# A gated mix of a convolution and a feed-forward net: first products over 512 tokens, another order of loads and of the merged work

## The chip, the core and the metric

The kernel runs on one core of a Trainium2 chip. The core has five engines that run side by side, each through its own list of instructions: TensorE (PE, matrix products, with weight loads shown apart as PEld), VectorE (DVE), ScalarE (ACT), GpSimd (POOL) and SyncE (SP, which here issues most DMAs). The metric is the device time of one execution in microseconds. Times of the kernel before are the median of 3 runs.

## What is computed

```python
x = A_u                                              # 1 x 2048 x 640
g = sigmoid((x * gate_w).sum(-1, keepdims=True))
a = A_ref(x, ...)     # S4D: a kernel K of 2048 taps for each of 640 channels,
                      # convolved with x by Fourier transforms, plus x * D_skip
b = relu(x @ w1) @ w2 # w1 640 x 1728, w2 1728 x 640
return g * a + (1 - g) * b
```

Three kinds of work follow from this: the generation of the taps K (exponentials and sines of 640 x 128 parameters), the convolution, and the feed-forward net `b`. Products are taken in three terms, with each operand split into a rounded part (`h`) and the rest (`l`): high x high, high x low, low x high.

## The kernel before

**Tiles and sweeps.** The hidden dimension of 1728 is cut into 13 tiles of 128 and one of 64. `PARTS = (5, 5, 4)` makes three sweeps `p` of 5, 5 and 4 tiles over all tokens; partial sums go to DRAM between sweeps. Tokens come in eight groups `g` of 256. For a group, first products (`hidden` or `wide`) give the hidden tiles, which ACT (`high`: relu, rounded) and DVE (`low`: the rest) evict from PSUM; second products (`sums`, four blocks j of 320 columns by 128 tokens) give the output.

**First sweep.** `hidden` (line 390) takes one group of 256 tokens and up to two tiles at a time; the hidden tiles are `h0`, `h2`, `h4`. The 64-wide tile (tile 13) is tile 0 of this sweep (line 248): its weights carry high and low side by side, so it needs two products in place of three, and a chain `fold`, `total`, `half_high`, `half_low` over ACT and DVE adds them. **Second and third sweep:** `wide` (line 453) takes 512 tokens, a pair of groups, one tile at a time. Rings in `ring(...)` count the buffers; `Token`s take and release them.

**x and the weights.** `load_x` (line 313) brings a group from DRAM, `trans` (line 335) transposes it on PE in three thirds of the model dimension, and ACT and DVE split it into `xx`. In the first sweep the transposes of group g+1 stand between the products of group g. `weights` (line 257) loads and splits w1 and w2; in the first sweep w1 comes as one load of 64 columns and two of 256. All of these loads are issued by SP.

**The parameters** (`params`, line 719) take 75 DVE steps, some ACT casts, stores to DRAM and loads of rows (`load_rows`), before the first block of the generation (`products`, line 910: PE on `tg,PS`) can start. Later come `factors` and `taps` (generation) and the stages of the convolution (`stage1`, `stage2`, `inv2`, `inv1`).

**The order** is written out by hand: every task is put in a queue such as `PE.ff` or `DVE.prma`, and the string `ORDER` (line 47) says from which queue the next task is taken, one letter a task (a digit repeats it). Each engine runs its tasks in that order. `Plan.run` (line 161) follows it, so nearly every instruction of the profile has line 185.

Of the kernel before, what the change touches and what calls it, by code (L numbers as in the profile page):

```python
# [11 lines left out]
F32 = mybir.dt.float32  # L12
# [16 lines left out]
HB = 1  # L29
# [17 lines left out]
ORDER = (  # L47
    '!PD;T4;mD;Da;Fan;Dn;aBmnmDBDcDBDmDmBD2a2naDnDBaDmDBmDnDBm2DBaDanDmnDBmW2DaBDanDnC2DaCDC!DCDa?2D?DaufuDS2uD2u'
    'DvaDv2Du!vDuDuvDaDa2uD2uDuDu2nDv2aDnDanDanDn3D2anDnv2DuDvaD2uDvDuveDCfDCDuD!DuWD2auDZaDvDuZD?uDvDaDa2nDu2aDn'
    'DnDvDuDavDanDu2DnD2avDnDnDw?DawDuDvDavDwDCgDCDu!DwD:DugD;Du;Du;DaWuD2aDauvDw2DuwuD2nDwauDwauDnanaDnDn2DawenD'  # L50
    'vaDv2DavDuDvWDawWngDvDwDvWDWvDf2Dava2DlWDW2DaDanlnDYDaYDanZnDZP2DaDanDnDEanDCbDCDbD!aDEnaoDbCDCbDo!bDtDt?DE?'
    'bpDpbpDbDpDbDpDaDpabp3DpDaoE2anGnbYbDqbt2DtDaDanDanDaoDbn2DnDabnDpEbpDpb2DpbDpDpDpaE2apDbDobGobn2tEqDbrpUDpb'
    'DpaDbDpDUDbpDbp2Dp2DpaE2aCGbroUbotDbD2nZDqZt2DU?aDananDYanDEnabnDpDbpDpDb2DpbDpbDpDp2DapaE2arDobCDbCDCbGont?'
    'EbtDpbDp2DpbDbp2DmspDbq2D2pDaDaEpamDb2nDsaoaDoGbtanbnEtDnBDbp;DBb2Dr;pbD,pDUbDpaDabpDpDUZpUDaDpmDmBEmoaG;b2B'
    'b;DUobqDqDtDbtDpDbpErbpUDbp2DbpDUZp;DpDmpD2aDnEaBmG;bBo;bDoYbtYDnXDnQDqbDpDrmtDmpDmBDaBDBDa!nDbnEXbspDQbDpDU'
    'bDpD2pDUDrpUEDobDbo!D2sbnDnUnG2tbnEpbDpbp2Dbq2DpbDoDpDpEpDbpDbnDnbDnoG2tbEqbDpb2rDU2pDbDbpDYDpZDpDpEpDboDboG'
    'nbtZtE;q2UDb2pDbpDbDspDbDpbDpDpDpD2aDnaEanGobYnXbnXDqbtDtDoDbpDpbE!pDabUDnDspb2DbpDpDpDpEDobnDnbGnb2tEoDbprp'
    'DUbpDbDpDb!DpbDpDp2DnqEZpDUb2rDUoboDbtGt2U2nEbpDpbpUDbDpbDpDbpDp2DqEnpDbnDboGZobYtXEqDrb2stDbpDpXbDpDbDpbDpD'
    'pDpD2aEpaDbYnUDobDnbDoGtUntbEpbD2pb2DpaDnDaDbnDpbDpDp2DpEnGnbrtUboDobqDtU!DEbp!DrpbUpDbDnbDnDpUb2DpDpDpDpEDn'
    'bnoDboDbDnqDrDtUbGt2bEUZpDpbnDpbDZp;D;DpDpEpDbpDbDoaDobG2tqEbnqDbpDpbDpDmpDmDmpDbBDapDarpU2DapDbDsn;DsnXDsnD'  # L60
    'aDnEtGrboBb;DbtUXDoUDqDrbpDpDb2UpDbDpmDUpDnD2nDnDpZDp2DpDBDB;Gn;nXDqDrsU2DnDUP2KQDQDnmDPmBZDmz;DzKzKQzDQz2Dz'
    'RDmzDaz2DaD2KzQDzQDBD.BDa.zD.DzXDsBDnDanL2nLAKAKADz2DzDzLALADRD2sAD!DADAD!DszDdDdnDndH2ndnH2hyHhyhDhyNhyDNDN'
    'yDNyHNHN2hyHhyhDhyNhyDNDnNnDyNDyHnNHhNhyIhyhyLNyNIA2NLA3iAIiA2LAIRADA2iZDAiZDiZDxZx2DaDnD2xHxH2hyHhyhHhyNhDy'
    'N2hDNyXDNyaDyNDyN-DxNxDNQxHanQHn2hyHhyhHhyNhJyh2NyNyJjyjOIhNyI+NKiN+iNizQKdzDiQdDzDXz2DKa!jnKz!LzdVLzdDA2DAD'
    'ADADL2nLAZDADA2DADMnDInIZQD2iDQiDiDVxD-xDRxDxDxDzDODM2n+DnHnx+Hh-hyHhyhZHhyNhyHN2hZNDy2hNyDxNDxNDyDyHyaNjyNH'
    'nhNHhy+hNhJyX2hyXNyNJjNyNyjINOI-K2iDizQiDzdKdONLzQzK+AD+A2Dz-KjzQLzjL+zdQLAdDRaADADVDAVDAIAIHiD2hyiDyiDinNDa'
    'xDMxHMxa!xNHhn+hHn!2hxDhyhDyDyNDxNDyDxDNxDNnDnHnyZHhyhHyN2hyJN2hNyNyHN2yJNhjyjOIhyI-Ki+2izKQizDOQzDjNDz+LNnN'
    'L+ANZLALAjDVADVAD-DAXDAMDKAMKzD2nDzDI2zInH2iH2hyHiyhiHyN2hHyN2hxDhOhyhNDy+NDxDNx+DNyZDyHyNyHNhnhNHy2hZNxDhyh'
    'DyN-DyaNDxNDyNDxyIxNIxNnJ3iIjIiOjJi-2iDXi+xDaxDdOxDdxDx-DxDx+DxjDn-DOD-Jj+2anJ+n-Dj2DOjVDVDO+3D+M2DVMDnVnj2D'
    'njDOnDdDMdM+DMk2DkZMnZDnDMDnMDk2ZDnkZ')  # L70
# [135 lines left out]
class Kernel:  # L206
# [29 lines left out]
    def feed_forward(self):  # L236
# [6 lines left out]
        for f in range(2, 5):  # L243
            ring(f"hw{f}", 1)
        for f in range(5):
# [11 lines left out]
        def weights(p, f, two, after=()):  # L257
# [7 lines left out]
            def load():  # L265
                if first:
                    n = 256 if f else fn
                    t = st['ws', key] = self.prm.tile([128, NT, n], F32, name=f"wq{f}")
                    D_.dma_start(t, io['B_w1'][:, f0:f0 + n].rearrange("(k p) f -> p k f", p=128))
                    if f:  # L270
                        st['ws', key], st['ws', (key[0], p, f + 1)] = t[:, :, :128], t[:, :, 128:]
# [1076 lines left out]
```

## Time and profile before

| | us |
|---|---|
| median of 3 runs | 611.13 (610.20 to 612.08) |
| the profiled execution | 611.85 |
| its span, first to last instruction | 610.1 |

```profile
PE 598.8 (98%) x8676; PEld 496.4 (81%) x8676; DVE 504.8 (83%) x841; ACT 379.7 (62%) x599; POOL 83.9 (14%) x114
...
PE   6999999999999999999999999999999999999996
PEld 6999998999998998898898896686757846757676
DVE  3788967899999999999998995898878867978542
ACT  4434458999999898899988852133352354343552
POOL 0000000000000000000000000016340360544525
PEclk9899999999999999999999999999999999999999
```

The first line is the busy time of each engine, its share of the span and its instructions. The rows below cut the span into 40 equal slices; a digit is the busy share in tenths, and `PEclk` the clock that TensorE was granted. PE is busy from the first slices to the last. The generation lies between about 94 and 368 us, where ACT and DVE are near full too; the convolution follows.

### The profile page before, as it was taken

How to read it: one execution, taken by the hardware profiler on the slowest of the kernel's cores; microseconds unless marked ns; L12 is line 12 of the kernel's file. 1: busy time of each engine (PE TensorE's matmuls, PEld its weight loads, DVE VectorE, ACT ScalarE, POOL GpSimd, SP SyncE). 2: the span in 40 equal slices, each digit the busy share in tenths (PEclk: the TensorE clock that was granted, in tenths of full speed). 3: DMA queues.
4: the chain of work that ended last, by engine and by line, in shares of the span. 5: the costliest groups of instructions: out<-in, count | busy, mean ns of one | idle time of the engine just before them, and what ended most of it. 6: DMA issues, size and time to landing. Idle time of an engine off the chain costs nothing.

```text
span 610.1 us, 20050 instructions
## 1 busy us (share of the span) xinstructions
PE 598.8 (98%) x8676; PEld 496.4 (81%) x8676; DVE 504.8 (83%) x841; ACT 379.7 (62%) x599; POOL 83.9 (14%) x114
## 2 busy tenths in 40 slices
PE   6999999999999999999999999999999999999996
PEld 6999998999998998898898896686757846757676
DVE  3788967899999999999998995898878867978542
ACT  4434458999999898899988852133352354343552
POOL 0000000000000000000000000016340360544525
PEclk9899999999999999999999999999999999999999
DMA  9767746406154824554155257982946969642376
GB/s 225 198 214 257 201 155 216 159 20 230 67 164 157 255 93 156 192 168 136 66 202 154 59 169 227 259 182 103 211 105 251 186 188 185 217 124 87 84 211 188
DMA packets 85697, 102.56 MB, mean 168 GB/s; under 512 B 28009, under 2 KB 68841, under 8 KB 85354
## 3 DMA queue, kind: packets, MB, share of 16 engines
q1 hardware_dynamic: 85210, 100.39, 55.9%
q8 instruction: 68, 1.11, 0.8%
q10 hardware_dynamic: 400, 0.90, 0.5%
q14 instruction: 19, 0.16, 0.1%
HBM read 62.21 MB, written 39.06 MB: 166 GB/s over the span
## 4 chain that ended last, share of the span: by engine, by line
PE 91%; DMA 3%; SPq 2%; POOL 1%; ACT 1%; issue 1%; DVE 0%; POOLq 0%; ACTq 0%
PE ps L185 91%; SPq L185 2%; DMA xu<-in_A_u_dram 1%; DMA out_dram<-yo 1%; POOL yo L185 1%; POOL q L185 1%; DMA xu<-part 1%; ACT yo L185 0%; ACT L185 0%; ACT mg L185 0%; ACT ku L185 0%; ACT q L185 0%; DVE q L185 0%; POOLq L1344 0%; ACTq L185 0%
## 5 line engine op out<-in xcount | busy, mean ns | idle before, releaser
L185 PE MATMUL ps<-xx,w1h 128*128 128x256 f32 (+1 forms) x760 | 185.3, 341 | 0.5 <-ACT xx L185 0.5
L185 PEld LDWEIGHTS ps<-xx,w1h 128*128 128x128 f32 x760 | 125.9, 191 | 22.5 <-issue 4.2
L185 POOL TENSOR_TENSOR ku<-kx 128x256 f32<-128x256 f32 x80 | 56.7, 738 | 462.5 <-DMA xu<-in_A_u_dram 408.4
L185 PE MATMUL ps<-xx,w1l 128*128 128x512 f32 (+1 forms) x340 | 116.2, 342 | 0.0
L185 ACT COPY ku<-ps 128x256 f32<-128x256 f32 (+1 forms) x120 | 47.9, 472 | 73.0 <-PE ps L185 72.6
L185 PE MATMUL ps<-w2h,hh 128*128 128x320 f32 x288 | 91.2, 320 | 0.0
L185 PE MATMUL ps<-w2l,hh 128*128 128x320 f32 x288 | 87.7, 308 | 0.4 <-issue 0.4
L185 DVE STREAM_TRANSPOSE ku<-ps 128x512 f32<-128x512 f32 x80 | 75.7, 1057 | 11.5 <-PE ps L185 11.4
L185 PE MATMUL ps<-w2h,hl 128*128 128x320 f32 x256 | 73.1, 311 | 0.0
L185 PEld LDWEIGHTS ps<-xx,w1l 128*128 128x128 f32 x340 | 65.0, 191 | 7.4
L185 DVE TENSOR_TENSOR kx<-ps,ku 128x512 f32<-128x512 f32 x80 | 50.6, 681 | 14.0 <-ACT ku L185 8.3
L185 PEld LDWEIGHTS ps<-w2h,hh 128*128 128x128 f32 x288 | 54.1, 188 | 8.4 <-DVE ku L185 2.8
L185 ACT ACT_TABLE_LOAD x42 | 53.9, 1283 | 0.7
L185 PEld LDWEIGHTS ps<-w2l,hh 128*128 128x128 f32 x288 | 54.1, 188 | 0.2
L185 DVE TENSOR_TENSOR mg<-mg,sc 128x1024 f32<-128x1024 f32 x40 | 49.0, 1225 | 3.6
L185 ACT COPY sc<-ps 128x1024 f32<-128x1024 f32 x40 | 40.3, 1008 | 16.7 <-PE ps L185 16.7
L185 DVE TENSOR_TENSOR sc<-sc,mg 128x1024 f32<-128x1024 f32 x40 | 48.6, 1216 | 0.0
L185 PEld LDWEIGHTS ps<-w2h,hl 128*128 128x128 f32 x256 | 46.5, 188 | 1.4 <-issue 0.9
L185 ACT ACTIVATE sc<-sc,half_pi 128x1024 f32<-128x1024 f32 x40 | 45.5, 1138 | 0.0
L185 ACT ACTIVATE sc<-sc 128x1024 f32<-128x1024 f32 x40 | 42.1, 1052 | 0.2
L185 ACT ACTIVATE mg<-ps 128x1024 f32<-128x1024 f32 x40 | 41.7, 1041 | 0.2
L185 PE MATMUL ps<-w2h,xu 128*128 128x320 f32 x160 | 39.7, 310 | 0.0
(161 smaller groups left out, 1090.0 us busy)
## 6 DMA issues: line engine op xcount, KB each, us to landing
xx<-xt SPq DMA_DIRECT2D x24, 640.0 KB, 8.2
xt<-xx SPq DMA_DIRECT2D x16, 640.0 KB, 6.6
part<-q SPq DMA_DIRECT2D x16, 640.0 KB, 4.3
q<-part SPq DMA_DIRECT2D x16, 640.0 KB, 5.5
ws<-in_B_w_dram SPq DMA_DIRECT2D x20, 320.0 KB, 4.1
kd<-kt SPq DMA_DIRECT2D x80, 64.0 KB, 2.8
ck<-kd SPq DMA_DIRECT2D x40, 128.0 KB, 3.4
xu<-in_A_u_dram SPq DMA_DIRECT2D x10, 512.0 KB, 8.2
```

The source lines that it names most:

```text
L185: return lambda *a, **k: self._tc.keep_in_program_order(f(*a, **k))
```

## The change

The diff does four things.

- **512 tokens from the third group on.** In the first sweep groups 0 and 1 keep `hidden`; groups 2 to 7 go through `wide` in pairs, in the order of tiles 4, 0, 1, 2, 3. `wide` learns the 64-wide tile (two products, then the fold chain for each half of the 512 tokens) and gets buffers in the first sweep: `h0` and `h2` as before, a new tile `h5`, two tiles of the convolution's `ck`, and `h4`. The transposes of a pair stand behind the pair before; they have queues of their own (`PE.tr`, `ACT.tr`, `DVE.tr`).
- **The half tile of w1 last.** The first sweep's tiles are now 0, 1, 2, 3, 13; w1 comes as loads of 128, 256, 128 and 64 columns.
- **The first x in three parts.** `load_first` issues each third as two DMAs, one on SP and one on ACT, with the first load of w1 between the second and the last third. In the first group the products of tiles 0 and 1 are split by term, so that the high x high term needs only the high parts.
- **A new merge order.** The whole string `ORDER` is replaced. It begins, in words: first two thirds of x, w1, last third, gate vector, the other w1 loads, second x, w2; on PE the transposes of x, all products of the first group, the transposes of the second group, its sums. The first block of the generation now stands in the products of groups 4 and 5, behind the first of the second tile's five steps; before, it stood behind all products of group 4.

```diff
-        nf = [(i * 128, min(128, DFF - i * 128)) for i in (13, *range(13))]
+        nf = [(i * 128, min(128, DFF - i * 128)) for i in (0, 1, 2, 3, 13, *range(4, 13))]
...
-                    n = 256 if f else fn
+                    n = 256 if f == 1 else fn
...
+        def load_first():
+            s_, ls = tok('xs'), []
+            for third in range(3):
+                def load(third=third):
+                    st['xs', 0], d = self.xu[:, 0], slice(256 * third, min(256 * third + 256, D))
+                    for h in range(2):
+                        (S if h else D_).dma_start(st['xs', 0][64 * h:64 * h + 64, :, d], xd[h, :, :2, d])
+                ls.append(A('SP', 'x0', load, take=() if third else [s_], use=[s_] if third else ()))
+            return s_, ls
...
+                if g == p == i == 0:
+                    nm = 2 if halves(p, f) else 3
+                    for m in range(nm):
+                        for third in range(3):
+                            new = r == third == m == 0
+                            x = X[0, 0][2 * third + (m == 1)]
+                            ts.append(A('PE', 'ff', early(r, f, third, m), [*(wt if nm == 2 else [wt[m == 2]]), x], take=[b_] if new else (),
+                                        use=[w_, xtok[0, 0]] + ([] if new else [b_])))
+                    continue
...
+                if p == 0 and f == 2:
+                    return [self.zp.tile([128, 512], F32R, name=f"h{x}5") for x in 'hl']
+                if p == 0 and f == 3:
+                    return [self.early.tile([128, 16, 32], F32R, name="ck", bufs=2).rearrange("p a b -> p (a b)") for _ in range(2)]
+                if p == 0:
+                    return [pa.tile([128, 2, 256], F32R, name="h4", bufs=1).rearrange("p a b -> p (a b)")]
...
-                    for m, (a, b) in enumerate(((wh, xh), (wh, xl), (wl, xh))):
-                        self.E.matmul(st['hb', 'w'], a[:, k], b, start=k == m == 0, stop=k == NT - 1 and m == 2)
+                    for m, (a, b) in enumerate(((wh, xh), (wh, xl), (wl, xh))[:nm]):
+                        self.E.matmul(st['hb', 'w'], a[:, k], b, start=k == m == 0, stop=k == NT - 1 and m == nm - 1)
...
+            if nm == 2:
+                x = ()
+                for t in range(2):
+                    z_ = tok('z')
+                    x = A('ACT', 'ff', lambda t=t: fold(t), [*ts, *x], take=[z_], use=[b_])
+                    x = A('DVE', 'ff', lambda t=t: total(t), [x], use=[b_, z_])
+                    x = A('ACT', 'ff', lambda t=t: half_high(t), [x], take=() if t else hs, use=[z_, *hs] if t else [z_])
+                    x = A('DVE', 'ff', lambda t=t: half_low(t), [x], use=[z_, *hs]),
...
-                q_ = tok('q')
+                q_, pair = tok('q'), p or g > 1
...
-                for k_, i in enumerate(range(0, 0 if p else n, 2)):
+                for i in () if pair else (4, 0, 2) if g else (0, 2, 4):
                     hidden(p, g, i, range(i, min(i + 2, n)))
...
+                if p == 0:
+                    for i in (1,) if g == 0 else (2, 3) if g == 1 else (g + 2, g + 3) if g % 2 == 0 and g < 6 else ():
+                        for third in range(3):
+                            trans(i, third, xs[i])
+                        if i < 7:
+                            xs[i + 1] = load_x(i + 1, [wload[0, PARTS[0] - 1, 1]])
```

More of the change, by code (lines that the diff above doesn't have):

```diff
@@ L297, in low @@
                 V.tensor_sub(l, t, w.bitcast(F32))
-            if first and f and f % 2 == 0:
+            if first and f == 2:
                 a, s_ = wload[p, f - 1, two], wq[f - 1]
@@ L423, in total, with room @@
                 V.tensor_add(st['z'], st['hb', i][:64, 0], st['z'])
+            def room():
+                if i < 4:
+                    st['h', i] = [pa.tile([128, 2, 256], F32R, name=f"h{x}{i}", bufs=1) for x in 'hl']
+                else:
+                    t = pa.tile([128, 2, 256], F32R, name="h4", bufs=1)
+                    st['h', i] = [t[:, x:x + 1] for x in range(2)]
             def high():
-                st['h', i] = [pa.tile([128, len(fs), 256], F32R, name=f"h{x}{i}", bufs=1 if i else HB) for x in 'hl']
+                room()
                 S.activation(st['h', i][0][:, lo:], st['hb', i][:, lo:len(fs)], AF.Relu)
@@ L433, in half_high @@
             def half_high():
+                room()
                 S.activation(st['h', i][0][:64, 0], st['z'], AF.Relu)
@@ L497, in sums @@
             ts_, ns = slice(t * 128, t * 128 + 128), slice(nh * 320, nh * 320 + 320)
-            if p:
-                hd, ht = zip(*HW[p, g // 2])
+            pair = p or g > 1
+            if pair:
+                hd, ht = zip(*(HW[p, g // 2][f] for f in range(n)))
+                ht = [x for y in ht for x in y]
             else:
```

124 lines of the change are left out of this document (72 added, 52 removed), and 17 rows, old and new, of the table QUEUES.

## The prediction

> **What bounds the kernel now.** I read the chain that ended last first, because it says which engine sets the time in each stage. Its pieces are start, length and what ran.
>
> ```profile
> span 610.1 us, 20050 instructions
> ...
> 14.91 79.74 PE ps L185 x609
> ...
> 98.13 269.87 PE ps L185 x4309
> ...
> 368.36 187.29 PE ps L185 x2859
> ```
>
> From 14.91 us to 555.65 us the chain is matmuls with almost nothing between them. The time is therefore the sum of what TensorE (PE) executes, plus the start and the few waits. A change counts by how much PE time it removes and by the waits it makes. Next I asked how close the other engines are, stage by stage. The columns after the span of each stretch are its length and the busy time of PE, weight loads, VectorE (DVE), ScalarE (ACT) and GpSimd, then clock and DMA.
>
> ```profile
> 5.13:8.55 3.42, 2.61 (x16) 1.79 (x16) 0.65 (x2) 1.43 (x3) 0.00 (x0) 1.00 1.10 287
> 8.55:11.96 3.41, 2.91 (x23) 2.58 (x22) 3.02 (x6) 2.22 (x4) 0.00 (x0) 1.00 1.12 297
> 11.96:15.37 3.41, 1.49 (x14) 1.32 (x12) 1.59 (x4) 2.42 (x5) 0.00 (x0) 1.00 0.99 236
> 15.37:18.79 3.42, 3.42 (x18) 3.42 (x17) 3.16 (x5) 2.56 (x4) 0.00 (x0) 0.50 1.10 342
> ...
> 27.60:85.65 58.05, 58.05 (x445) 57.81 (x444) 49.56 (x109) 25.34 (x53) 0.00 (x0) 1.00 0.65 211
> 93.77:156.14 62.37, 61.28 (x1003) 57.42 (x1002) 56.06 (x100) 59.85 (x76) 0.00 (x0) 1.00 0.42 143
> 156.14:226.05 69.91, 69.91 (x1123) 62.65 (x1117) 68.03 (x114) 65.61 (x77) 0.00 (x0) 1.00 0.50 155
> ```
>
> The first generation stage (93.77 to 156.14) has ACT busy for 59.85 of 62.37 us, the second DVE for 68.03 of 69.91. PE is the bound there by only 2 us. In the start the DMA engines are full until 12 us, PE was idle for over half of 11.96:15.37, and the next stretch ran at clock 0.50.
>
> **The change part by part.** All sums go against the profiled execution, 611.85 us (span 610.1 and 1.75 around it); the median of the runs is 611.13, 0.72 lower, and the forecast is put there.
>
> *First: 512 tokens at once.* Six of the eight groups of the first sweep are affected. Each had 4x15 + 10 = 70 matmuls of 256 columns (the half tile has two products), so 420 become 210 of 512 columns. What one of each costs is the distance of starts:
>
> ```profile
> 31.13 1.60 PE L185 MATMUL ps<-xx,w1h 128*128 128x256 f32 x12
> 32.57 0.28 PE L185 MATMUL ps<-xx,w1l 128*128 128x256 f32 x1
> ...
> 181.76 0.63 PE L185 MATMUL ps<-xx,w1h 128*128 128x512 f32 x2
> ...
> 182.45 0.63 PE L185 MATMUL ps<-xx,w1h 128*128 128x512 f32 x2
> ...
> 229.73 0.62 PE L185 MATMUL ps<-xx,w1h 128*128 128x512 f32 x2
> 230.19 0.39 PE L185 MATMUL ps<-xx,w1l 128*128 128x512 f32 x1
> 230.41 0.62 PE L185 MATMUL ps<-xx,w1h 128*128 128x512 f32 x2
> ...
> 232.23 0.39 PE L185 MATMUL ps<-xx,w1l 128*128 128x512 f32 x1
> 232.54 0.50 PE L185 MATMUL ps<-tg,PS 32*128 32x512 f32 x4
> ...
> 233.32 0.73 PE L185 MATMUL ps<-xx,w1h 128*128 128x512 f32 x2
> 233.89 0.40 PE L185 MATMUL ps<-xx,w1l 128*128 128x512 f32 x1
> ```
>
> (32.57 - 31.13)/12 = 0.120 us for 256 columns; (230.41 - 229.73)/3 = 0.227 for 512. Two small ones cost 0.240, so a merged pair saves 0.0133 us and 210 pairs save **2.8 us**. In the last stretch 233.32 to 233.89 the distance is 0.285 a piece because a packed block stands before it, which is the next term. Another run has (182.45 - 181.76)/3 = 0.23, by which the saving is 2.1; I take 2.8, since most starts are 0.227 apart like the later run. All of it lies on the path.
>
> By the Trainium skill ("TensorE: Matmul & The Clock Gate", section Back-to-back issue gap) a warm matmul takes its columns at 2.4 GHz and about 2.5 ns, so an estimate by the Trainium skill is 210 x 2.5 ns = 0.5 us saved instead of 2.8. The rows give 13 ns, and no run here shows 2.5; a stream with a weight load in front of every matmul evidently pays more.
>
> *Second: the merge order.* I read the two order strings and counted, for PE, how often a run of feed-forward matmuls is broken by the packed work (generation, convolution): 67 times before, 65 after. One break costs 232.54 - 232.23 - 0.227 = 0.08 going out and 233.89 - 233.32 - 2 x 0.227 = 0.12 coming back, together 0.2 us. Two fewer save **0.4 us** (at least 0, as they may go into convolution runs). ACT and DVE evict four full tiles of a pair instead of six pieces; they work beside PE, which sets the time, so I cost that at nothing; it gives them a little room where they are near full.
>
> *Third: the start.* These rows carry it.
>
> ```profile
> 0.73 0.60 SPq L185 DMA_DIRECT2D xu<-in_A_u_dram  x1
> ...
> 9.39 3.01 SPq L185 DMA_DIRECT2D wo<-in_B_w_dram  x2
> ```
> ```profile
> 9.73 1.67 PE L185 MATMUL ps<-xx,w1h 128*128 128x256 f32 x12 [0.50 <-ACT xx L185]
> ...
> 14.91 0.67 PE L185 MATMUL ps<-ident,xu 128*128 128x128 f32 x4 [1.92 <-DMA xu<-in_A_u_dram]
> 15.30 0.72 PE L185 MATMUL ps<-xx,w1h 128*128 128x256 f32 x2
> ...
> 22.84 0.39 PE L185 MATMUL ps<-w2h,hh 128*128 128x320 f32 x1
> ...
> 24.97 0.31 PE L185 MATMUL ps<-w2h,hh 128*128 128x320 f32 x1
> ```
> ```profile
> 13.72 0.37 ACT L185 COPY z<-ps 64x256 f32<-64x256 f32 x1
> 14.91 0.42 ACT L185 ACTIVATE hh<-z 64x256 fp32r<-64x256 f32 x1 [0.81 <-DVE z L185]
> ...
> 21.63 1.37 ACT L185 CAST w2h<-wo 128x640 fp32r<-128x640 f32 x2
> ```
> ```profile
> 14.47 0.41 DVE L185 TENSOR_TENSOR z<-ps,z 64x256 f32<-64x256 f32 x1
> ...
> 22.50 1.55 DVE L185 TENSOR_TENSOR w2l<-wo,w2h 128x640 fp32r<-128x640 f32 x2
> ```
> ```profile
> wo<-in_B_w_dram SPq DMA_DIRECT2D x2, 320.0 KB, 7.4
> ```
> ```profile
> ck<-kd SPq DMA_DIRECT2D x40, 128.0 KB, 3.4
> ```
>
> Before, PE does 25 matmuls, waits 1.92 us for the second x, then runs at half clock. After, the second x is used only behind all 70 matmuls of the first group: from about 9 us (as before, 9.73, less what the first third brings) 70 x 0.120 = 8.4 us, to 17.5, with its 10 transposes ((15.30 - 14.91)/4 = 0.10 each) at about 18.5. The wait for x is gone, and what is late next is w2. Its last tile was issued by 12.40 and landed 7.4 us after issue, near 19.5, and the same bytes stand ahead of it (x, the same 576 columns of w1, x again). Three DMAs for x instead of one on SP and ACT cost two more issues of 0.60 us each; w1, the gate vector, the second x and w2 queue behind them, but the DMA engines are full then, so they hide it. ACT must cast five w2 tiles (1.37/2 = 0.7 each) behind the last eviction of the first group (17.5 + 0.37 + 0.41 + 0.42 = 18.7, the three steps of the half tile), and DVE needs 0.8 behind each: the last is ready near 22.4. The second block of sums then starts near 23.3 against 24.97, 1.7 us earlier. But PE has meanwhile waited some 2 to 3 us between 18.5 and 22.4. A stretch with PE busy for 1.49 of 3.41 us was followed by one at clock 0.50, which costs half of 3.4, 1.7 us. I expect that again, so the start saves **0.1 us**; ends: 1.7 saved, or 0.5 lost if more and smaller packets delay w2.
>
> The Trainium skill ("TensorE: Matmul & The Clock Gate", Part 1, What's actually happening) says that the clock halves after an idle window of about 3.4 us. In this trace it halved after a stretch that was 44% busy. Were the rule strict, the 1.7 us would be kept; that is a rival below.
>
> *Fourth: new waits.* The new order puts the first generation block (PE on `tg,PS`) earlier.
>
> ```profile
> 84.83 0.82 DVE L185 TENSOR_TENSOR hl<-ph,hl 128x640 fp32r<-128x640 f32 x1 [0.79 <-ACT hl L185]
> ```
> ```profile
> 88.94 0.91 SPq L185 DMA_DIRECT2D PS<-ps  x2
> ```
> ```profile
> 93.77 0.51 PE L185 MATMUL ps<-tg,PS 32*128 32x512 f32 x4
> ...
> 98.13 0.50 PE L185 MATMUL ps<-tg,PS 32*128 32x512 f32 x4 [1.08 <-ACT mg L185]
> ```
>
> Between 31.13 and 93.77 PE has 62.6 us of work. The new order drops three groups' products (3 x 70 x 0.120 = 25.2) and puts in one pair (70 x 0.227 = 15.9), 13 more wide matmuls (3.0) and two transposes (0.2): 56.5 us, so PE is there at 31.0 + 56.5 = 87.5, 6.3 us earlier. The block needs the parameters: DVE's last step ended at 84.83 + 0.82 = 85.65, was stored, and its load was issued at 88.94; with some 2 us for the landing (3.4 of `ck<-kd` above is the long end) the round trip is 6.2 us. To be in time the parameters must end at 81.3. DVE was busy 49.56 of the 58.05 us from 27.60 to 85.65; in the new list it does all 75 parameter steps in that part and about 1 us less of the rest. 27.6 + 48.5 = 76.1 without any wait; 5.2 us of waits are allowed where there were 8.5. Part of those were waits for feed-forward work that comes sooner now. I count **0.5 us** lost here. Then the second block waits for ACT as before (1.08), behind 9 x 0.227 = 2.0 us of cover instead of 14 x 0.152 (22.84 to 24.97) and two transposes, 2.3: **0.3 us** lost, including what ACT costs PE up to the tenth block (end: 2.5, below). Queued behind a waiting PE is everything. The tail is unchanged within 0.6 us: the last convolution blocks stand one task later and the sums behind them are the same.
>
> Sum: -2.8 - 0.4 - 0.1 + 0.5 + 0.3 = -2.5, so 611.85 - 2.5 = 609.35 as a profiled execution and **608.6** as a median.
>
> **The rivals.**
> *Start at full clock.* The pause at w2 doesn't halve the clock and the parameters keep up: 1.6 more, 607.0. For it: the pause is split into pieces. Against: the row at 0.50. Chance 0.13.
> *Generation bound.* Up to the tenth block PE's work falls by 3 us (62.37 to about 59), while ACT's 59.85 falls by 0.5. PE then waits for ACT, up to 2.5 us, and most of the gain is given back: 611.1. For it: both rows above. Against: ACT's 59.85 includes work that belongs to later blocks. Chance 0.20.
> *Fixed cost isn't saved.* If the columns alone set the pace, 2.8 goes: 611.4. The rows speak against it. The Trainium skill's 2.5 ns would come near this. Chance 0.04.
> *Parameters late, slower.* The parameters end no earlier than before, at 85.65, since they hang on stores and ACT casts in a row. Then the first block starts at 88.94 + 3.4 = 92.3, PE waits 4.8 us, and the next 3.4 us run at half clock, 1.7: -2.5 - 0.5 + 4.8 + 1.7 = +3.5, 614.6. It decides from a parameter end of 81.3 + 3.0 = 84.3, where the wait alone eats the gain. For it: DVE's 85% there. Chance 0.10.
>
> **How the numbers follow.** The forecast has 0.53 and covers 607.3 to 610.0. About 0.3%, 1.8 us, is what a measurement of this kernel can tell from no change. Below 609.3: the forecast's larger part (0.42) and the full-clock start (0.13), 0.55. Within: the rest of the forecast (0.11), the two rivals that give the gain back (0.22): 0.33. Above 612.9: 0.12. The range takes in the full-clock start with the larger savings (-2.8 - 0.4 - 1.7 = -4.9, 606.2) and generation with the smaller ones (-2.1 + 0.5 + 2.5 = +0.9, 612.0).
>
> **What would show it.** Starts of the wide matmuls of the first sweep 0.227 apart, and 210 of them; PE's second sums block near 23.3 us with a clock of 0.50 somewhere in 22 to 26; the first generation block near 88 us with an idle time before it under 1 us; no wait of PE for ACT over 1 us up to 150 us. Wrong if PE waits at the first generation block for more than 3 us, if the start shows x or w1 late, or if ACT's waits for PE vanish and PE's for ACT appear.

## The result and the profile after

The change made the kernel slower, by half a percent. The median is 613.59 us (611.18 to 617.00, 20 runs) against 610.86 us (608.77 to 612.99, 20 runs) for the kernel before: a ratio of 1.0052, with a 95% interval of 1.0036 to 1.0068. The forecast of 608.6 and its range up to 612.0 both miss. The profiled execution took 612.75 us, one of the quicker ones, with a span of 610.9.

The summary lines of the changed kernel's page, to be set against those of the kernel before:

```profile
span 610.9 us, 19586 instructions
...
PE 597.5 (98%) x8466; PEld 484.9 (79%) x8466; DVE 503.1 (82%) x833; ACT 379.0 (62%) x591; POOL 83.8 (14%) x114
...
PE   8999999999999999999999999999999989999997
```

PE has 210 matmuls fewer (8676 to 8466), as the change says, and is busy for 1.3 us less, yet the span is 0.8 us longer. So something else ate what the fewer products saved. The chain that ended last says where to look (start, length, what ran):

```profile
24.71 64.22 PE ps L186 x420
...
111.78 2.98 ACT sc L186 x3
...
158.16 12.16 PE ps L186 x210
...
206.38 4.99 ACT sc L186 x5
...
244.55 254.73 PE ps L186 x3869
499.28 1.65 issue
500.93 71.83 PE ps L186 x1305
```

Before, one unbroken piece of PE work ran from 98.13 to 368. Now the chain runs through ACT and DVE between 90 and 244 us, and PE stops for 1.65 us at 499.28 with nothing that the profile shows it to wait for. The third place is the start. This table holds the times (us) at which marks of the program are reached:

| | before | after |
|---|---|---|
| second block of sums of the first group | 24.97 | 25.54 |
| first block of the generation | 93.77 | 88.05 |
| last pair of taps | 365.22 | 363.79 |
| end of PE's work | 604.98 | 606.76 |

The stretch between the second and the third mark grew from 271.45 to 275.74 us, 4.3 us, of which PE's own work is 1.3 (270.37 to 271.69, busy). The stretch from the last taps to the end grew by 3.2. The pause is 1.65 of it; most of the rest is work, since 26 products more stand there (3743 before, 3769 after; PE busy 239.4 and 241.2 us). The windows of the changed kernel's start (columns as in the prediction):

```profile
5.13:8.55 3.42, 2.94 (x16) 2.17 (x16) 1.26 (x2) 1.52 (x4) 0.00 (x0) 1.00 1.02 282
8.55:11.96 3.41, 3.41 (x16) 2.96 (x15) 2.17 (x5) 2.00 (x4) 0.00 (x0) 0.65 1.18 264
11.96:15.37 3.41, 3.41 (x27) 3.41 (x26) 1.94 (x3) 2.38 (x4) 0.00 (x0) 0.85 1.03 219
15.37:18.79 3.42, 3.42 (x31) 3.42 (x30) 0.69 (x1) 0.44 (x1) 0.00 (x0) 1.00 1.07 305
20.46:25.54 5.08, 3.67 (x16) 2.29 (x15) 5.02 (x8) 4.25 (x8) 0.00 (x0) 1.00 1.14 304
```

PE is busy without a gap from 8.55 to 18.79, so the wait for the second x is gone. But the clock fell early instead, between 8.55 and 15: (1 - 0.65) x 3.41 + (1 - 0.85) x 3.41 = 1.7 us lost. From 20.46 PE waits for w2, piece by piece:

```profile
20.46 0.41 PE L186 MATMUL ps<-w2h,hh 128*128 128x320 f32 x1
21.19 0.41 PE L186 MATMUL ps<-w2l,hh 128*128 128x320 f32 x1 [0.32 <-DVE w2l L186]
...
22.50 0.41 PE L186 MATMUL ps<-w2l,hh 128*128 128x320 f32 x1 [0.56 <-DVE w2l L186]
...
25.54 0.31 PE L186 MATMUL ps<-w2h,hh 128*128 128x320 f32 x1
```

One loss of 1.7 us in 611 is a mean clock of 0.997, which is what this execution shows. The other runs of the changed kernel have a median clock of 0.994 (two such losses would give 0.9944), and time goes with it: 611.18 us at 0.999, 613.3 to 614.4 at 0.994, 616 to 617 at 0.990. The kernel before has 0.9955 to 0.997. So three causes are to be told apart: the waits at the start and the clock, the merge order in the generation, and the pause.

### The profile page after: what moved, and what is told of

Its sections match the earlier page's. It is cut to its first block, busy times and chain, and to the rows that moved or that the text cites. A ratio compares the mean times of both kernels' runs of the same rounds, so it can differ in the third digit from the quotient of the medians.

```text
span 610.9 us, 19586 instructions
## 1 busy us (share of the span) xinstructions
PE 597.5 (98%) x8466; PEld 484.9 (79%) x8466; DVE 503.1 (82%) x833; ACT 379.0 (62%) x591; POOL 83.8 (14%) x114
## 3 DMA queue, kind: packets, MB, share of 16 engines
q8 instruction: 66, 1.08, 0.7%
## 4 chain that ended last, share of the span: by engine, by line
PE 74%; ACT 12%; DVE 9%; issue 2%; DMA 1%; SPq 0%; POOL 0%; DVEq 0%; ACTq 0%; POOLq 0%
PE ps L186 74%; ACT sc L186 5%; ACT L186 3%; DVE sc L186 2%; DVE mg L186 2%; ACT mg L186 2%; DVE G L186 2%; DVE w2l L186 1%; DMA xu<-in_A_u_dram 1%; ACT q L186 1%; DVE hl L186 1%; ACT yo L186 0%; SPq L186 0%; DMA out_dram<-yo 0%; ACT w1h L186 0%
## 5 line engine op out<-in xcount | busy, mean ns | idle before, releaser
L186 PE MATMUL ps<-xx,w1h 128*128 128x512 f32 (+1 forms) x610 | 175.7, 380 | 0.5 <-DVE hl L186 0.3
L186 PEld LDWEIGHTS ps<-xx,w1h 128*128 128x128 f32 x610 | 108.7, 191 | 26.6 <-issue 1.8
L186 PE MATMUL ps<-xx,w1l 128*128 128x512 f32 (+1 forms) x280 | 104.2, 377 | 0.0
L186 ACT COPY ku<-ps 128x256 f32<-128x256 f32 (+1 forms) x120 | 47.7, 462 | 79.0 <-PE ps L186 78.8
L186 PE MATMUL ps<-w2h,hh 128*128 128x320 f32 x232 | 74.1, 321 | 0.7 <-DVE hl L186 0.7
L186 PE MATMUL ps<-w2l,hh 128*128 128x320 f32 x232 | 71.7, 311 | 1.2 <-DVE w2l L186 1.2
L186 PE MATMUL ps<-w2h,hl 128*128 128x320 f32 x232 | 67.1, 313 | 0.0
L186 PEld LDWEIGHTS ps<-xx,w1l 128*128 128x128 f32 x280 | 52.7, 191 | 9.9
L186 DVE TENSOR_TENSOR kx<-ps,ku 128x512 f32<-128x512 f32 x80 | 50.4, 681 | 12.1 <-POOL ku L186 8.7
L186 PEld LDWEIGHTS ps<-w2h,hh 128*128 128x128 f32 x232 | 43.5, 188 | 9.5 <-DVE ku L186 2.8
L186 PEld LDWEIGHTS ps<-w2l,hh 128*128 128x128 f32 x232 | 43.6, 188 | 2.4 <-DVE w2l L186 2.2
L186 PEld LDWEIGHTS ps<-w2h,hl 128*128 128x128 f32 x232 | 42.2, 188 | 2.1 <-issue 1.6
```

Of the source, the lines that this page charges most:

```text
L186: return lambda *a, **k: self._tc.keep_in_program_order(f(*a, **k))
```

## The experiments

Times below are medians, ratios are against the kernel before on the same chip, and brackets hold the 95% interval. A letter in an expectation names a theory as that expectation tells it.

### The waits at the start and the clock

**Filling the waits (e1).** Products of the identity into an unused bank stand where PE would wait: three among the first transposes, nine between the products that wait for w2. They compute nothing that is used.

```diff
+    def fill(self, n):
+        for _ in range(n):
+            self.E.matmul(self.ps[:, 3, :128], self.ident, self.ident, start=True, stop=True)
...
+                if g == 0:
+                    self.fill((1, 2, 0)[third])
...
+                        if p == g == j == 0:
+                            self.fill({0: 2, 1: 1, 2: 3, 4: 1, 6: 1, 8: 1}.get(k, 0))
```

> The changed kernel with nine short products of the identity, results unread, and three more in PE's waits at the start (5.9 to 9.4 us and 20.5 to 24.7 us). Theory C (clock): the waits in pieces at the start let the granted clock fall to half in most runs, in a stretch or two more than the profiled one, and this is some 1.8 us of the 2.7 us lost. Then the mean clock of the runs rises from a median of 0.994 to 0.997 or more and the time falls by 1.5 to 2.5 us against the changed kernel (to 611 to 612 us, ratio to the kernel before 1.000 to 1.002). Rival O (order: all the loss is PE waiting for DVE and ACT in the generation): clock and time stay, 613 to 614 us, ratio 1.004 to 1.006.

Measured: 610.76 us, ratio 0.9998 [0.9985, 1.0011]; the median clock is 1.000, where it was 0.994. Twelve products that do nothing take 0.5% off, a little more than theory C said. Its windows show PE busy throughout and the clock at 1.00 where the unfilled kernel had 0.65 and where it had waited for w2:

```profile
8.55:11.96 3.41, 3.41 (x23) 2.71 (x22) 2.29 (x4) 2.31 (x5) 0.00 (x0) 1.00 1.16 281
11.96:15.37 3.41, 3.41 (x31) 3.41 (x30) 2.44 (x4) 2.32 (x5) 0.00 (x0) 1.00 1.02 222
...
18.79:24.61 5.82, 5.82 (x42) 5.18 (x40) 5.50 (x9) 4.59 (x9) 0.00 (x0) 1.00 1.04 249
```

**Filling only the waits for w2 (e8).**

```diff
-                    self.fill((1, 2, 0)[third])
+                    self.fill(0)
```

> The kernel of e1 with the filling products in the waits for w2 alone (20.5 to 24.7 us), none among the first transposes. Theory C1 (the second stretch of half clock comes from the waits for w2): mean clock 0.997, 611.3 to 612.3 us, between e1 and the changed kernel, ratio 1.001 to 1.003. C2 (both stretches come from the first waits): clock 0.994 to 0.995 and 613 to 614 us, ratio 1.004 to 1.006. C3 (the first waits do nothing): clock 0.999 or more and 610.5 to 611 us.

Measured: 609.96 us, 0.9986 [0.9972, 1.0000], median clock 0.9985, between C1 and C3 in the clock and quicker than each of the three numbers. The waits for w2 alone carry the gain. Its profiled execution still has the early fall (0.63 and 0.86 in the two windows from 8.55 to 15.37), so the fall that goes is the one behind w2's waits. Not all of the gain need be the clock's: the added products also shift PE's list of instructions, and the profiles of e1 and e8 lack the pause at 499 us and have another, of 1.42 and 0.57 us, at 133 to 135 us (the last part of the experiments is on these pauses).

**The same on the kernel before (e2).** Fourteen fills: four more ahead of x, two behind the transposes of the first x, eight in the wait for the second x.

```diff
-SPIN = 10
+SPIN = 14
...
+                if (g, third) == (0, 2):
+                    self.fill(2)
...
+                    if p == g == i == 0 and (r, third) == (1, 2):
+                        self.fill(8)
```

> The kernel before with fourteen short products of the identity, results unread, in its waits at the start (4 more ahead of the first transpose, 2 at 9.1 us, 8 in the 2.1 us from 12.84 us on). Theory C: the half-clock stretch of 3.4 us that follows the wait costs 1.7 us; with the wait filled it goes, and the kernel gains 1 to 1.7 us (ratio 0.997 to 0.998). Rival: the stretch comes from the first microseconds, whatever stands in this wait: ratio 1.000 within 0.001.

Measured: 612.00 us, 1.0018 [1.0004, 1.0033]: a miss. The clock rose to 0.9985 and the time did not fall. In its profile the marks are 1.8 us ahead up to about 115 us and the lead is lost behind, 1.1 of it around a pause of 0.74 at 180 us. So a start that is earlier isn't kept as such.

**Second x behind w2 (e9).** The load of the second x is moved behind w2's, and its transposes behind the first group's first sums, so that w2 lands earlier.

```diff
-        xs[1] = load_x(1, q='w')
...
+        xs[1] = load_x(1, q='w')
```

> The changed kernel, no filling products, with the second x loaded behind the five tiles of w2 instead of ahead of them, its three transposes behind the first sums block, and the casts of w2 ahead of the rectifiers that wait for PE. The generation's order is the changed one. Theory S (the last tile of w2 lands 2.3 us later than in the kernel before, at 21.75 us; PE waits for w2 in pieces and the clock falls behind it): the second sums block then starts at 22.5 to 23.5 us instead of 25.54, the mean clock of the runs rises to 0.996 or more, and the kernel takes 609.5 to 611.3 us (ratio 0.998 to 1.001), 2.3 to 4 us less than the changed kernel. Rival: the loads share the same bandwidth, so that something else is late instead (the second x, the parameters): the first block of the second group or the first generation block comes no earlier than in the changed kernel, and the time stays at 613 us or more.

Measured: 612.31 us, 1.0030 [1.0016, 1.0044]. The second block of sums started at 25.91: a miss. w2's third tile landed at 15.41 and was cast at 19.16, because its cast stood behind work that waited for PE. The order on ACT and DVE held it, not the load. Its windows show what a wait for w2 does to the clock:

```profile
20.00:24.00 4.00, 2.79 (x14) 1.86 (x14) 3.04 (x5) 1.93 (x4) 0.00 (x0) 1.00 1.01 237
24.00:27.00 3.00, 3.00 (x16) 3.00 (x14) 1.20 (x2) 1.87 (x4) 0.00 (x0) 0.51 1.05 410
```

PE was busy for 2.79 of 4.00 us, in pieces, and then ran at 0.51 for three. This is the second fall. In the changed kernel's own profile it happens not to be there. Three other profiles have the changed kernel's start as it is. That of e3 (below) has both falls, the second one right behind the waits for w2:

```profile
10.47:13.88 3.41, 3.41 (x19) 3.41 (x18) 2.11 (x3) 2.29 (x4) 0.00 (x0) 0.50 1.07 212
...
20.50:24.12 3.62, 2.56 (x12) 1.41 (x10) 3.56 (x6) 3.27 (x6) 0.00 (x0) 1.00 0.99 258
24.12:27.54 3.42, 3.24 (x12) 2.95 (x12) 3.42 (x7) 1.43 (x4) 0.00 (x0) 0.50 1.08 414
```

That of e13 has the second fall alone, and that of e4 neither. So the same start has no fall, one or two, from one execution to the next: the median clock of the runs is 0.994 for the changed kernel and 0.997 for e4. That the median run of the changed kernel has both is read from its clock.

### What the wide products give

**Two of 256 columns again (e3, e7).** Everything of the change is kept, but each product over 512 tokens of the first sweep is issued as two over 256 into the same bank. e3 does it in the changed kernel, e7 in e1.

```diff
-                        self.E.matmul(st['hb', 'w'], a[:, k], b, start=k == m == 0, stop=k == NT - 1 and m == nm - 1)
+                        for c in (slice(0, 256), slice(256, 512)) if p == 0 else (slice(0, 512),):
+                            self.E.matmul(st['hb', 'w'][:, c], a[:, k], self.xx[:, m == 1, c.start // 256, k] if p == 0 else b,
+                                          start=k == m == 0 and not c.start, stop=k == NT - 1 and m == nm - 1 and c.stop == 512)
```

> The changed kernel with each product over 512 tokens of the first sweep issued as two over 256 into the same bank, all else and the order kept. 210 pairs cost 2.6 to 2.8 us of PE work more. Theory O (PE waits for DVE and ACT in the generation, so PE work there is partly free): 1.0 us more ahead of the first generation block, and the waits of the generation fall by most of the 1.6 us added in it: 0.9 to 1.5 us slower than the changed kernel (614.5 to 615.1 us, ratio 1.006 to 1.009). Rival B (PE alone bounds it, the products' saving is in the time in full): 2.6 to 2.8 us slower, 616.3 us, ratio 1.009 to 1.010. Rival W (the wide products themselves bring the waits): no slower or faster than the changed kernel.

> The kernel of e1 with each product over 512 tokens of the first sweep issued as two over 256, order kept. In e3 this cost 8 us beside the changed kernel where the work explains 2.6 us; half clock and pauses that no engine ends were seen there. If these were the clock's (theory C) and the merge is worth its 2.6 us of work or less, then with the waits filled the clock stays at 0.998 or more and the kernel is 1.0 to 2.6 us slower than e1: 611.8 to 613.4 us, ratio 1.002 to 1.005. Rival P: with more instructions PE's supply of instructions fails more often wherever they stand; then it is slower by 4 us or more again, 614.8 us or more, ratio 1.007 or more.

Measured: e3 621.95 us, 1.0174 [1.0149, 1.0199], outside every theory's number. e7 615.68 us, 1.0076 [1.0061, 1.0091], 4.9 us above e1, as rival P had it. By the median distances of starts (0.120 and 0.227 us) the products account for 2.7 us of it, about what the prediction had. For the other 2.2, e7's profile shows 2.6: a pause of 2.33 us at 150 us, where e1's is 1.42, and half clock for 3.41 us behind it, 1.7 us. Two runs of e7 at a clock of 1.000 still took 614.17 and 615.88 us, so in the runs it isn't all the clock's. What fills e3's 8 us is partly seen: its profile has seven places where PE stops and waits for nothing, 5.7 us together. The longest, in its timeline:

```profile
276.69 0.32 PE L186 MATMUL ps<-mg,sc 128*32 128x64 f32 x2 [2.42 <-issue]
```

and a window behind it, where PE runs at 0.50:

```profile
277.00:278.00 1.00, 1.00 (x19) 0.74 (x13) 0.64 (x1) 1.00 (x2) 0.00 (x0) 0.50 0.00 0
```

So part "First" of the change is worth having: taking it out costs at least what it was to save.

### The merge order

**Another order for 85 to 366 us (e4).** Found by a search over orders, with in-order engines and the durations of the trace. Only the string differs.

> The changed kernel with the same instructions in another merge order from 85 to 366 us (some of DVE's, ACT's and PE's work moved by a few places so that what PE waits for comes earlier; nothing ahead of the first generation block is touched). Theory O: the waits of PE in the generation come from the order alone; the stage from the first to the last generation block falls from 275.7 us by 2 to 4 us, and the time by 2 to 3 us (610.5 to 611.6 us, ratio 0.999 to 1.001). Rival D (DVE's and ACT's load is the bound whatever the order): the stage stays within 0.7 us and so does the time. Rival C alone: no change either.

Measured: 613.75 us, 1.0053 [1.0034, 1.0072]: no gain, a miss. The reason shows in DVE's timeline of e4:

```profile
182.31 1.22 DVE L184 TENSOR_TENSOR sc<-sc,mg 128x1024 f32<-128x1024 f32 x1
188.05 0.72 DVE L184 STREAM_TRANSPOSE kt<-ps 128x512 f32<-128x512 f32 x1 [4.52 <-ACT hh L184]
```

DVE stood idle for 4.52 us before the transpose of a pair's taps. That transpose reads the bank that was named last when its turn in the order came. Where the order puts it behind the next pair's products (`taps`), it reads those, in place of its own pair's, and waits until they are done. The profile names ACT as the one that ended the wait; that it was PE's products is read from the code and shown by e5. The search had not known of this wait. The changed order has the transpose in such a place at pairs 5, 7 and 9, the kernel before at 4, 14 and 16, and e4's at 5. By the code this is an error and not only a wait: three pairs of 32 channels each get the taps of the pair behind them, in the kernel before as in the changed one. The orders of e5, e6, e10, e11, e12 and e15 are free of it. The same step in the changed kernel's DVE timeline:

```profile
186.60 0.67 DVE L186 TENSOR_TENSOR mg<-mg 128x512 f32<-128x512 f32 x1
...
188.19 0.72 DVE L186 STREAM_TRANSPOSE kt<-ps 128x512 f32<-128x512 f32 x1 [0.93 <-ACT w2h L186]
```

**Those three transposes first (e5).** e1 with three letters moved: `r` (the transpose) ahead of `I` (the next pair's products). The two other places look the same as this one.

```diff
-qanGnpIaubrnoF
+qanGnprIaubnoF
```

> The kernel of e1 (changed kernel with PE's waits at the start filled) with three transposes of a generation pair's result moved ahead of the next pair's products (pairs 5, 7 and 9). In the changed order they stand behind those products, take the bank that these name, and so wait for them: DVE stands 1 to 3 us late there. Theory O (DVE's and ACT's place in the order makes PE wait): some 1.5 us of the generation's 4.3 us come back, 609.0 to 609.6 us, ratio 0.997 to 0.999. Rival D (the generation ends when DVE and ACT have done their sum of work): no gain, 610.3 to 611 us, ratio 0.999 to 1.001.

Measured: 608.90 us, 0.9973 [0.9955, 0.9991], as the order theory had it. In its DVE timeline the transpose starts at 186.11 us without a wait.

The windows from the first block of the generation to the last pair of taps, first e1's row, then e5's, say how much that is:

```profile
87.11:363.98 276.87, 271.68 (x4169) 235.25 (x4168) 256.69 (x431) 244.31 (x271) 0.00 (x0) 1.00 0.44 142
```
```profile
86.67:361.49 274.82, 271.34 (x4168) 235.19 (x4167) 256.70 (x431) 244.39 (x271) 0.00 (x0) 1.00 0.45 143
```

2.05 us are gained with nearly the same work on every engine. A pause inside this stretch, at product 1238, is 0.7 us of it (1.42 us in e1, 0.73 in e5), so the transposes are worth some 1.4 us in the profiles. In the ratios the three moved letters are worth 0.25%, 1.5 us.

**A new order with every transpose in its place (e6).** e1 with an order for 88 to 366 us found by a search that knows of the wait, and w2's first cast earlier. Only the string differs from e1.

> The kernel of e1 with the same instructions in another merge order from 88 to 366 us, every transpose ahead of the next pair's products, and the first cast and subtraction of w2 moved ahead of the rectifier of the third and fourth tile at the start. Theory O: the stage from the first to the last generation block falls from 275.7 to 276.9 us to 271.5 to 273 us, the second sums block starts 0.5 to 0.8 us earlier, and the time falls by 3.5 to 5 us against e1, to 606 to 607.5 us (ratio 0.993 to 0.995). Rival D: the stage stays over 275 us and the time over 609.5 us.

Measured: 607.75 us (606.84 to 608.43), 0.9951 [0.9937, 0.9964]: the best of all versions, 3 us ahead of the kernel before. Its row for the same stretch:

```profile
86.62:359.89 273.27, 270.32 (x4165) 234.52 (x4164) 255.45 (x427) 244.39 (x271) 0.00 (x0) 1.00 0.45 144
```

3.6 us less than e1's row, 1.36 of it busy time and some 1.0 a shorter pause (0.45 us, where e1 has 1.42). w2's early cast gave 0.1 us only: the other tiles' casts still stood behind the half tile's chain.

**The same search on the kernel before (e11).**

> The kernel before with the same instructions in another merge order from 88 to 366 us, found in the same way as that of e6, every transpose ahead of the next pair's products. If the order of the changed kernel was the poorer one (theory O), this brings the kernel before little, 0.5 to 1.5 us (609.0 to 610.3 us, ratio 0.997 to 0.999), against the 3 us of e6 over e1. If any order found this way wins as much, 607 to 608 us, ratio 0.995 or less, and e6 says nothing of the changed order in particular.

Measured: 610.76 us, 1.0001 [0.9988, 1.0014]. The kernel before gains nothing from it, less even than theory O allowed. So, as far as one search can show, the changed order was the poorer one, and it isn't that any order could have been bettered.

### Start and order together

**No fills, but the loads of e9 and the order of e6 (e10); then all five casts of w2 ahead of the half tile's chain too, with the half tile's five products last in the first block of sums (e12).**

```diff
-                prod.sort(key=lambda x: x[1])
+                prod.sort(key=lambda x: (p == g == 0 and x[0] == 4, x[1]))
```

> The start of e9 with the merge order of e6 from 88 to 366 us; no filling products. Both theories (start and order) together: e6 without its filled waits, and its second sums block 1 to 2 us earlier: 605.5 to 607.3 us, ratio 0.991 to 0.995. If the clock needed the filling products, 608 us or more.

> The merge order of e6 from 88 to 366 us and, at the start, e9's loads (w2 ahead of the second x) with all five casts and subtractions of w2 ahead of the third and fourth tile's rectifier, and the half tile's five products last in the first sums block instead of in the middle. No filling products. In e9 PE still waited in pieces from 20 to 24 us, since three of w2's tiles were cast behind work that waits for PE, though they had landed, and the clock fell right behind (0.50 from 24 to 27 us). Theory S in this form (the casts' place, not the landing, sets the wait): the second sums block starts at 22.8 to 23.8 us (25.9 in e9, with the three transposes ahead of it in both), no half clock after 20 us, mean clock 0.996 or more, and 606 to 607.8 us, ratio 0.992 to 0.996. Rival (PE waits for w2's landing all the same): the second sums block at 25 us or later, half clock behind it, and 610.5 us or more as in e10.

Measured: e10 611.25 us (607.52 to 615.69), 1.0010 [0.9988, 1.0033], a miss. Its clock is 0.994 as in the changed kernel, since the waits for w2 stayed, and its runs scatter by 8 us. e12 607.99 us, 0.9969 [0.9956, 0.9981], just above its range, with the rest as theory S had it: the median clock is 0.9965, the second block of sums starts at 23.44, and the windows show the wait for w2 gone and no fall behind it:

```profile
20.00:24.00 4.00, 3.33 (x25) 3.00 (x25) 1.81 (x5) 1.96 (x5) 0.00 (x0) 1.00 1.15 289
24.00:28.00 4.00, 4.00 (x29) 4.00 (x29) 4.00 (x10) 1.01 (x4) 0.00 (x0) 1.00 0.85 325
```

So the change is good for a gain of 0.3% without any added work, once the start and the order are put right, and of 0.5% with e1's fills.

### The pause at 499 us

The profiles of after, e4, e9, e10 and e12 all stop PE at the same place of the program, ahead of its product number 6842 (6843 in e12), for 1.2 to 1.8 us. The changed kernel's timeline of PE:

```profile
497.26 2.03 PE L186 MATMUL ps<-ku,tn 32*64 32x128 f32 x121
500.93 0.44 PE L186 MATMUL ps<-ku,tn 32*64 32x128 f32 x7 [1.65 <-issue]
```

In e12 a fall of the clock follows it, as the window behind it shows:

```profile
498.00:500.00 2.00, 2.00 (x12) 0.69 (x8) 1.43 (x2) 1.30 (x5) 2.00 (x4) 0.50 0.43 120
```

Other profiles stop at other products: 5066 (before, 0.36), 2516 (after, 0.31), 1238 (e1, e5 and e8: 1.42, 0.73, 0.57), 1622 (e7, 2.33). The seven stops of e3 are at 1622, 1877, 3154, 3538, 3792, 4176 and 4815. Counted from the first, that is 255, 1532, 1916, 2170, 2554 and 3193 products, or 2, 12, 15, 17, 20 and 25 steps of 127.5 to 127.7. The same numbers come back in other kernels with other work at them: 1622 in e7, 1877 and 3792 in e4, 4176 in e10, e12 and e15.

With PE's weight loads and semaphore instructions counted too, the step is exact. All 28 stops of over 0.2 us for which the profile names no cause, in the seventeen profiles together, stand 193 or 194 records behind a multiple of 256. The traces also hold the transfers that bring instructions, on a queue of their own. Its row on the changed kernel's page:

```profile
q8 instruction: 66, 1.08, 0.7%
```

These are 66 packets of 16 KB for PE's 17035 records, one for about 258. Each of the 28 stops ends 1.2 to 1.5 us after such a packet has landed: the stop at 499.28 ends at 500.93, its packet came from 498.02 to 499.50. Packets are 9 us apart on average, so this is no chance. PE waits there for its next block of instructions. Why the packet is late at 28 edges of blocks and not at some 1040 others is open. PE had run through the block ahead in under 4.8 us in 27 of the 28 cases (the median block takes 8.0), but some 200 blocks as short had no stop behind them.

**Shifting the stream (e13, e14, e15).** One-column products of the identity are put ahead of the convolution, so that the same instruction has another number: 12 in the changed kernel (24 records), 23 in the kernel before, 12 in e12. They compute nothing that is used.

```diff
+                if k and i == q == 0:
+                    for _ in range(12):
+                        self.E.matmul(self.ps[:, bs[0].slot, :1], self.ident, self.ident[:, :1], start=True, stop=True)
```

> The changed kernel with 12 one-column products of the identity (24 records), results overwritten, ahead of the convolution's first products. In every kernel of 8466 products PE stops for 1.2 to 1.8 us at product 6842, in the last products of a burst of 128 short ones in the convolution; in the kernel before and in those with 18 or more products added it does not. Theory P (PE's instructions come in blocks of about 128 products, and the change's 210 fewer products moved a block's edge to the end of that burst): the pause goes, PE gains 1.2 to 1.8 us there for at most 0.7 us spent on the added products, and, where the granted clock fell behind that pause, up to 1.7 us more: 611.3 to 613 us, ratio 1.001 to 1.004. Rival (the pause belongs to that place in the program, for instance to its transfers): it stays, and the time is 613.5 to 614.3 us, ratio 1.005 to 1.007.

> The mirror: the kernel before with 23 one-column products of the identity (46 records) ahead of the convolution's first products, so that its products stand to the blocks of 128 from there on as those of the changed kernel do (8676 + 46 is 8466 and twice 128). Theory P: a pause of 1.2 to 1.8 us appears in the burst at 495 to 497 us, which had none; with 0.8 to 1.3 us for the added products 612.3 to 613.8 us, ratio 1.003 to 1.006. Rival: only the added products' own time, 611 to 611.8 us, ratio 1.001 to 1.002.

> e12 with the 12 products of e13. Theory P: e12's profile has a pause of 1.75 us at product 6843 and 3.4 us of half clock behind it; both go, 606 to 607.2 us, ratio 0.991 to 0.995. Rival: 608 to 608.7 us.

Measured: e13 613.14 us, 1.0047 [1.0025, 1.0068]; e14 628.11, 1.0291 [1.0266, 1.0317]; e15 611.63, 1.0008 [0.9989, 1.0027]. In e13 and e15 the pause is gone from its place, which takes some 2.0 and 2.1 us off there. But the added products cost far more than the 0.7 us expected, and all three runs miss on that. e13's windows over them, over the 16 products behind them, and on:

```profile
370.33:373.44 3.11, 3.11 (x26) 3.10 (x24) 0.49 (x1) 0.00 (x0) 0.00 (x0) 0.84 0.11 32
373.44:377.06 3.62, 3.62 (x17) 0.79 (x16) 0.00 (x0) 0.00 (x0) 0.00 (x0) 0.50 0.07 14
377.06:380.00 2.94, 2.94 (x17) 2.94 (x14) 0.00 (x0) 0.00 (x0) 0.00 (x0) 0.63 0.71 185
```

The 24 records take 3.11 us, and the 16 convolution products behind them 3.62 where the changed kernel needs 1.88, at half clock. So the pause depends on where an instruction lies in the stream, as e1, e5, e6 and e8, with 18 or 24 records more, had shown already. What it costs in a run without a profile they don't show, as the added products drown it.

The mirror, e14, does not bear theory P out: no stop came in the burst that the kernel before runs at 495 to 497 us. Its profile has stops at products 6843 (1.76 us, for which the profile names a DMA, at the same place of a block and 1.5 us behind a packet) and 7349 (4.51 us). Together they make up the time: against the kernel before, the added products and half clock for 6.83 us cost some 8 us, the first stop 2.0 and the second, with half clock for 6.83 us more, 7.5.

## Why the prediction was wrong, by its own steps

**First: right in mechanism and in size.** The wide products start (90.32 - 89.63)/3 = 0.23 us apart, and the median distance is 0.120 us for 256 columns and 0.227 for 512 in both kernels. So 420 products were 50.4 us and 210 are 47.7, 2.7 less against a forecast of 2.8. The changed kernel's timeline:

```profile
89.63 0.62 PE L186 MATMUL ps<-xx,w1h 128*128 128x512 f32 x2
90.09 0.39 PE L186 MATMUL ps<-xx,w1l 128*128 128x512 f32 x1
90.32 0.62 PE L186 MATMUL ps<-xx,w1h 128*128 128x512 f32 x2
```

The rival by which a fixed cost isn't saved falls: the trace shows some 13 ns a product (2.7 us over 210). The Trainium skill ("TensorE: Matmul & The Clock Gate", section Back-to-back issue gap) gives the 2.5 ns for an isolated product, and here a weight load stands ahead of each, so the estimate from it in the prediction was too low.

**Second: failed.** The step counted the breaks of a run of products on PE (67 to 65) and gave the rest of the order nothing, as ACT and DVE "work beside PE". The quoted rows had DVE at 68.03 of 69.91 us; a wait put into DVE there is a wait of PE. PE's idle time in the generation, stops aside, grew from 1.1 to 3.6 us. Three transposes that wait for the next pair's products are 1.4 us of this by the profiles of e1 and e5, 1.5 to 1.9 in the runs. The order of e6, which has none of them, wins back 2.6 in the profiles without the stop.

**Third: failed.** Forecast 0.1 saved; found 0.6 lost in the profiled execution and one more fall of the clock in the median run. The wait for the second x did go. But w2's last tile was issued at 13.63 (before at 12.07) and took 8.1 us (7.4 before), so that it landed at 21.75 and not near 19.5. The row of its issues in the DMA view:

```profile
wo<-in_B_w_dram SPq DMA_DIRECT2D x2, 160.0 KB, 8.1
```

"But the DMA engines are full then, so they hide it" is what fails: issued 1.6 us later, the tile landed 2.3 us later. The sum itself also had a slip: 18.7 for the last eviction, five casts of 0.7 and 0.8 for DVE make 23.0 for the last tile of w2, not 22.4. The half clock of 1.7 us came, but early, behind the first transposes' waits (0.65 and 0.85 from 8.55 to 15), and the waits for w2, 1.4 us in five pieces, bring a second one in many runs. The Trainium skill ("TensorE: Matmul & The Clock Gate", Part 1, What's actually happening) ties the fall to an idle window of about 3.4 us; e9's 0.51 behind 2.79 busy of 4.00 us, and e13's behind a stretch with no idle time at all, speak against it as a full rule. (Busy is the profile's count here: a product of one column counts too.)

**Fourth: right where it looked, and it looked too short.** The first block of the generation came at 88.05 (forecast 87.5 to 88) with no wait for the parameters, so that rival falls. The second block waited for ACT:

```profile
88.05 0.50 PE L186 MATMUL ps<-tg,PS 32*128 32x512 f32 x4
...
92.41 0.51 PE L186 MATMUL ps<-tg,PS 32*128 32x512 f32 x4 [1.23 <-ACT mg L186]
```

1.23 against 1.08 before. Up to the tenth block, at 149 us, PE's waits for ACT on this tile sum to 1.65 us, so the rival of a bound there, with up to 2.5 us, shows in kind but falls short in size. Behind the second block, up to 245 us, PE has six more waits of 0.25 to 0.71 us, 2.4 us together, three of them for DVE (1.4). The step stopped at the tenth block. That the tail is unchanged within 0.6 us failed too: it grew by 3.2.

**Not foreseen:** the pause ahead of product 6842.

How the sum comes out in the two profiled executions, whose mean clock is the same: -2.7 (products) + 0.6 (start) + 2.6 (PE's waits in the generation) + 1.6 (stops: 1.65 and 0.31, less the 0.36 of before) = +2.1, where PE's work ends 1.8 us later. Behind it the changed kernel is 1.0 us quicker to its end, so that the execution is 0.9 longer. With one more fall of the clock, 1.7, that is 2.6; the medians differ by 2.7. A straight line through time against clock, drawn to full clock, gives about 610.7 for the changed kernel's runs against 609.4 for those of the kernel before, +1.3. The terms of products, start, transposes and clock are shown by rows and experiments. That the stop at 499 us costs its 1.65 us in runs without a profile too is argued, not shown.

## What to carry to other kernels

When an order of merged work is replaced, follow the engine that is nearest to PE (here DVE, 97% busy in one stage) through the whole stage, and ask of each of its steps which buffer it reads and whose work it thereby waits for: three letters were worth about half of what 210 merged products saved. At the start, count what a moved load's issues do to the last load in the queue, and treat short waits of PE as costing their length and a share of a fall of the clock. Twelve products without a use, put into such waits, took 0.5% off the changed kernel; in the kernel before, fourteen took nothing off.

## What the runs showed of the hardware

- The clock halves behind short broken waits, not only behind a long idle stretch: 0.51 for 3 us behind 2.79 busy of 4.00 (e9), 0.50 behind a pause of 1.75 us at 496 us (e12), and 0.50 from 372.4 to 379.3 us behind 24 one-column products, which the profile counts as busy throughout (e13). It doesn't always: the changed kernel's own pause of 1.65 us had none behind it. In the seventeen traces each fall ahead of the end lasts 3.41 us or twice that, and 3.41 us cost about 1.7.
- PE can stop at the edge of a block of 256 of its instructions until a 16 KB packet of the instruction queue has landed: 28 stops of 0.2 to 4.5 us, each ending 1.2 to 1.5 us after the packet. Adding 24 records ahead of a stop removed it from its place. Which edges are hit is open.
- A one-column product isn't cheap: 24 records took 3.11 us, 0.13 us each, at a mean clock of 0.84.
